# Another planned order of jobs for a three-layer block on one core: new seeds, other assumed transfer times

## The chip, the cores and the metric

The kernel runs on one core of one Trainium2 chip. The metric is the device time of one execution in microseconds (us), as the median of several runs. TensorE is PE in the profile, VectorE is DVE, ScalarE is ACT, GpSimd is POOL and SyncE, which here only issues DMAs, is SP.

## What is computed

Three layers run one after the other on 4 batches of 576 positions. The first is masked attention with 8 heads of 64 (half of them see a window of 32 positions, the other half every 32nd position), the second a gated feed-forward layer with a shift by one position, the third a feed-forward layer with a convolution of width 3 and a sigmoid gate.

```python
attn = softmax(where(mask, q @ k.T / 8, -1e9)) @ v          # 4 batches x 8 heads, 576 x 64
x_prev = shift_by_one(x)
xk = mu_k * x + (1 - mu_k) * x_prev;  xr = mu_r * x + (1 - mu_r) * x_prev
x = sigmoid(xr @ w_r) * (relu(xk @ w_k) ** 2 @ w_v)         # 512 -> 1024 -> 512
h = relu(x @ w_in)
c = conv_w[0] * h[t-1] + conv_w[1] * h[t] + conv_w[2] * h[t+1]
out = (h * sigmoid(c)) @ w_out                              # 512 -> 1024 -> 512
```

The weights of layers two and three arrive as 64-bit floats.

## The kernel before

Every matrix product is made of passes of 128 x 128 weights against 288 columns (half a batch, called a chunk; there are 8). For accuracy each operand is split into a high and a low part, and a product takes three passes instead of one. The weights are read as 64-bit words in pieces of 512 KB (tiles `raw`), which ScalarE or VectorE narrow to 32 bits (`wb`, `wt`, lines 407 to 418) and split (`wkh`, `wkl` and so on, lines 457 and 458).

There are two stages, and each is planned and emitted as a whole. In the first stage attention of batch b (scores `sc`, line 590; maximum and mask on VectorE, line 606; exponentials on ScalarE, line 611; turning the probabilities with TensorE, `tr`, lines 634 and 644; values `pv`, lines 667 and 676) stands beside the products of layer two (`mm`, line 785, with weights `wr`, `wk`, `wv`). Beside this the weights of layer three are prepared: read, narrowed, combined for a scheme with seven products in place of eight, split into `ws` (lines 471 and 472) and stored to DRAM (`wi_d`, `wo_d`). The results of layer two are split into `xo` (lines 852 and 853) and stored to DRAM too (`x_d`). In the second stage layer three runs: products `hh` (line 1038) from blocks `x` that are loaded back, and products `oz` and `ov` (line 1135).

Buffers are few: 2 of `raw`, 3 of `ws`, 2 of `xo`. An operation that writes into a `ws` or `xo` waits until the transfer out of the same buffer's earlier content has landed; an operation that reads `raw` waits for its transfer in. VectorE and ScalarE work through their instructions strictly in the order in which they were emitted, so what stands behind such a waiting operation waits too.

That order is set by a planner in the kernel file, which runs when the program is built. `Plan.run` (line 249) goes through the jobs with a list of estimated costs: at each step it takes the job that can start first, with ties broken by a rank. For a transfer it uses one line of estimated time with a fixed latency and a rate (line 316):

```python
dma = max(dma, t + DMA_LATENCY) + j.nbytes / DMA_RATE
j.end = dma
```

`Plan.search` (line 231) starts from ranks that follow the longest path, and then applies a fixed chain of seeds (the table `STEPS`, one tuple for each stage); each seed moves the ranks of some jobs by pseudo-random amounts (`vary`, line 191). The order of the last plan is what is emitted, and with it which of ScalarE and VectorE does a job that both can do. Where the plan has TensorE idle for over 0.48 us in its first 60 us, filling passes are emitted that compute nothing of use (`stir`, line 952): as many as `int((idle - 0.3) / 0.17)`, or `/ 0.26` near the start (line 292). `COLD` is the time until which the planner counts TensorE as slow.

The names of tiles in the order listings below carry a number where two words meet, as in `x_1_5969`; the number rises with the place of the job in the plan, and a higher one is a later job.

Of the kernel before, what the change touches and what calls it, by code (L numbers as in the profile page):

```python
# [26 lines left out]
BANKS = {"sc": 2, "tr": 2, "pv": 1, "mm": 3}  # L27
WARM, MIXES, BEHIND = 10, 2, (0, 3)
REBIAS = 2.0 ** -112
DMA_RATE, DMA_LATENCY = 365.0e3, 2.0  # L30
FOREVER = 1.0e9
PREFER, PREFER_FROM, BESIDE = 0.5, 20.0, 0.3
QUEUE, FEED = 64, 0.0142
CHUNK, AHEAD, FETCH, CROWD = 256, 85, 4.4, (0.4, 6.0)
GAP = {("mm", "half"): 0.09, ("tr", "half"): 0.17, ("tr", "tr"): 0.08}
ENTER = {("half", "mm"): 0.11, ("tr", "mm"): 0.085, ("half", "tr"): 0.05}
STEPS = ((30100000002, 30100000004, 30100000014, 30100000016, 30100000078, 30100000091, 30100000108, 30100000115, 30100000116, 30100000143,
# [9 lines left out]
HALF_ARRAY = {"sc", "pv"}  # L47
BLOCKS = ("B11", "B21", "B22", "T4", "T1", "T2", "T3")
WEIGHTS = ("A11", "A12", "A22", "S3", "S4", "S1", "S2")
# [7 lines left out]
SCRATCH = 1024  # L57
TAIL = 20.0
LQ, LK, LW, LB, LEAD = 64, 64, 96, (5, 4), 3
STIR_UNTIL, COLD = 60.0, 6.0  # L60
BANKED = {"sc", "tr", "pv", "mm"}
RIGHT = {"raw", "ws", "wt", "wb", "qk", "vt", "pr", "nmx", "sums", "rec", "pt"}
LATENCY = {"PE": 0.22, "ACT": 0.16, "DVE": 0.12, "POOL": 0.12, "SP": 0.0}
# [273 lines left out]
def block_kernel(ctx, tc, qkL, qkS, vL, vW, vS, mu_k, mu_r, w_k, w_v, w_r, w_in, conv_w, w_out, ident, mask_l, mask_w, mask_s, out):  # L337
# [612 lines left out]
    def stir(n, into, anew=True):  # L950
        for _ in range(n):
            pe.matmul(into[:, :T], idle[:, :P], idle, start=anew, stop=anew)
# [46 lines left out]
    def issue(stirred=False):  # L999
        plan.stirred = stirred  # L1000
        with tc.manual_schedule():
            if stirred:
                stir(WARM, scrap)
            for job, e, start, end in plan.search(START if stirred else SECOND, STEPS[not stirred]):
                if e == "PE":
# [282 lines left out]
```

## Time and profile before

| | |
|---|---|
| median of 3 runs | 515.7 us (513.41 to 516.38) |
| time of the profiled execution | 515.84 us |
| its span on the chip | 514.1 us |
| TensorE busy | 97% of the span |
| VectorE busy | 83% |
| ScalarE busy | 76% |
| moved by DMA | 96.61 MB, mean 188 GB/s |

The time of the profiled execution is 1.74 us longer than its span, for what lies around the span. Busy time says that an engine holds an instruction. TensorE is the engine nearly always busy, so the reading starts from the few places where it is not, and goes from each of them back to what released it.

### The profile page before, as it was taken

How to read it: one execution, taken by the hardware profiler on the slowest of the kernel's cores; microseconds unless marked ns; L12 is line 12 of the kernel's file. 1: busy time of each engine (PE TensorE's matmuls, PEld its weight loads, DVE VectorE, ACT ScalarE, POOL GpSimd, SP SyncE). 2: the span in 40 equal slices, each digit the busy share in tenths (PEclk: the TensorE clock that was granted, in tenths of full speed). 3: DMA queues.
4: the chain of work that ended last, by engine and by line, in shares of the span. 5: the costliest groups of instructions: out<-in, count | busy, mean ns of one | idle time of the engine just before them, and what ended most of it. 6: DMA issues, size and time to landing. Idle time of an engine off the chain costs nothing.

```text
span 514.1 us, 13571 instructions
## 1 busy us (share of the span) xinstructions
PE 498.6 (97%) x5123; PEld 480.7 (94%) x5123; DVE 424.9 (83%) x1195; ACT 390.6 (76%) x1140; POOL 1.1 (0%) x15
## 2 busy tenths in 40 slices
PE   8889999999999999999999999999999999999997
PEld 5679999899998899999899999999999999999997
DVE  4899899898946998977899613679999997897993
ACT  6999998999647999948979535377778667676762
POOL 0000000000000000000000000000000000000000
PEclk9999999999999999999999999999999999999999
DMA  8965575855676873797345997348109104610111
GB/s 289 368 197 158 171 242 181 283 199 193 206 241 210 328 254 126 244 311 254 132 165 205 364 312 250 118 170 292 42 13 345 46 25 160 219 38 1 47 48 69
DMA packets 57921, 96.61 MB, mean 188 GB/s; under 512 B 4864, under 2 KB 41984, under 8 KB 57600
## 3 DMA queue, kind: packets, MB, share of 16 engines
q1 hardware_dynamic: 57568, 95.58, 54.5%
q8 instruction: 40, 0.66, 0.6%
q14 instruction: 25, 0.20, 0.1%
q10 hardware_dynamic: 288, 0.16, 0.1%
HBM read 63.95 MB, written 31.78 MB: 186 GB/s over the span
## 4 chain that ended last, share of the span: by engine, by line
PE 56%; DMA 17%; ACT 14%; DVE 10%; issue 2%; SPq 0%; DVEq 0%; ACTq 0%
PE mm L785 22%; PE hh L1038 15%; PE oz L1135 10%; PE ov L1135 7%; DMA wi_d<-ws 3%; DMA wo_d<-ws 3%; DMA x_d<-xo 2%; ACT pr L611 2%; DMA raw<-in_w_r 2%; DMA raw<-in_w_v 2%; ACT mx L764 1%; DMA vt<-in_vW 1%; ACT wb L407 1%; DVE ws L472 1%; DMA x<-x_d 1%
## 5 line engine op out<-in xcount | busy, mean ns | idle before, releaser
L785 PE MATMUL mm<-X,wvh 128*128 128x288 f32 x448 | 83.2, 297 | 0.0
L1038 PE MATMUL hh<-x,wi 128*128 128x288 f32 x504 | 76.0, 297 | 1.4 <-DMA x<-x_d 0.7
L1038 PEld LDWEIGHTS hh<-x,wi 128*128 128x128 f32 x504 | 69.8, 188 | 2.8 <-DVE hb L1050 0.9
L785 PE MATMUL mm<-Y,wkh 128*128 128x288 f32 x384 | 69.0, 296 | 0.2 <-DVE sq L815 0.2
L785 PEld LDWEIGHTS mm<-X,wvh 128*128 128x128 f32 x448 | 66.7, 188 | 0.3
L611 ACT ACTIVATE pr<-pr,nmx 128x54 f32<-128x54 f32 (+2 forms) x160 | 53.6, 346 | 4.8 <-DVE nmx L606 4.8
L785 PEld LDWEIGHTS mm<-Y,wkh 128*128 128x128 f32 x384 | 56.5, 188 | 0.7 <-DVE sq L815 0.4
L785 PE MATMUL mm<-Y,wrh 128*128 128x288 f32 x256 | 55.2, 298 | 1.0 <-ACT rs L797 1.0
L1092 DVE SCALAR_TENSOR_TENSOR graw<-hb,cw_sb,graw 128x576 f32<-128x576 f32 x64 | 51.5, 812 | 1.6 <-ACT graw L1087 1.0
L1110 ACT ACTIVATE blk<-graw 128x576 fp32r<-128x576 f32 x56 | 37.4, 681 | 14.9 <-DVE graw L1094 4.1
L785 PE MATMUL mm<-X,wvl 128*128 128x288 f32 x224 | 47.9, 295 | 0.0
L1111 DVE TENSOR_TENSOR blk<-graw,blk 128x576 fp32r<-128x576 f32 x56 | 41.5, 752 | 6.0 <-ACT blk L1110 5.5
L785 PEld LDWEIGHTS mm<-Y,wrh 128*128 128x128 f32 x256 | 42.2, 188 | 1.7 <-ACT rs L797 1.5
L785 PE MATMUL mm<-Y,wkl 128*128 128x288 f32 x192 | 40.9, 294 | 0.0
L785 PE MATMUL mm<-Y,wrl 128*128 128x288 f32 x128 | 37.9, 296 | 0.3 <-DVE wrl L458 0.3
L826 DVE TENSOR_TENSOR X<-sq,X 128x288 fp32r<-128x288 f32 x48 | 21.5, 454 | 18.8 <-ACT X L824 14.9
L785 PEld LDWEIGHTS mm<-X,wvl 128*128 128x128 f32 x224 | 35.9, 188 | 0.0
L611 ACT ACTIVATION_READ_ACCUMULATOR pr<-pr,nmx 128x1 f32 x160 | 32.0, 200 | 0.0
L785 PEld LDWEIGHTS mm<-Y,wkl 128*128 128x128 f32 x192 | 30.6, 188 | 0.0
L1135 PE MATMUL oz<-blk,wo 128*128 128x288 f32 x192 | 30.1, 296 | 0.0
L808 ACT ACTIVATE rl<-mm 128x288 f32<-128x288 f32 x64 | 25.3, 404 | 6.3 <-PE mm L785 5.3
L472 DVE TENSOR_TENSOR ws<-wt,ws 128x512 fp32r<-128x512 f32 (+1 forms) x32 | 19.8, 619 | 9.9 <-DMA wi_d<-ws 5.4
(162 smaller groups left out, 1240.4 us busy)
## 6 DMA issues: line engine op xcount, KB each, us to landing
x_d<-xo SPq DMA_DIRECT2D x42, 288.0 KB, 2.5
x<-x_d SPq DMA_DIRECT2D x21, 576.0 KB, 6.0
wi_d<-ws SPq DMA_DIRECT2D x24, 256.0 KB, 4.0
wo_d<-ws SPq DMA_DIRECT2D x24, 256.0 KB, 2.6
wi<-wi_d SPq DMA_DIRECT2D x6, 896.0 KB, 7.8
qk<-in_qkS SPq DMA_DIRECT2D x8, 599.0 KB, 5.1
out<-ob SPq DMA_DIRECT2D x32, 144.0 KB, 1.7
qk<-in_qkL SPq DMA_DIRECT2D x7, 592.0 KB, 5.9
```

Source lines behind the costliest of these rows:

```text
L407: act.activation(b(), hw, AF.Copy, scale=REBIAS)
L472: plan.add({"DVE": 0.07 + n / 960}, lambda e: dve.tensor_tensor(lo()[:, :n], t()[:, k], hi()[:, :n].bitcast(F32), ALU.subtract), [t, hi], ...
L611: act.activation(pr()[:, k], pr()[:, k], AF.Exp, bias=nmx()[:, i:i + 1], scale=-1.0, accum_out=sums()[:, i:i + 1])
L764: plan.add({"ACT": 0.225 + n_ / 1400}, lambda e, v=v, t=t: act.activation(v(), x()[:, t, 1 + o:1 + o + n_], AF.Copy, scale=mu[:, t:t + 1]) ...
L785: pe.matmul(o(), w_cols(name, j, t, part), x_[t](), start=(t == 0 and part == 0 and x_ is xhi), stop=(t == nk - 1 and x_ is xlo))
L808: plan.add({"ACT": 0.295}, lambda e: act.activation(r(), o(), AF.Relu), [o], [r])
L826: plan.add({"DVE": 0.37}, lambda e: dve.tensor_tensor(l_(), sq(), h_().bitcast(F32), ALU.subtract), [sq, h_], [l_])
L1038: pe.matmul(o(), w(hw, j), x()[:, hx, j], start=anew and n == 0 and j == 0, stop=last and n == 2 and j == 1, skip_group_check=True)
L1092: plan.add({"DVE": 0.735}, lambda e, k=k: dve.scalar_tensor_tensor(c(), h()[:, k:k + S], cw_sb[:, k * NF + f:k * NF + f + 1], c(), ALU.mul ...
L1110: plan.add({"ACT": 0.13 + S / 1400}, lambda e, w=w, x=x: act.activation(w()[:, 0], x(), AF.Copy), [mine], [(w, 0)])
L1111: plan.add({"DVE": 0.07 + S / 960}, lambda e, w=w, x=x: dve.tensor_tensor(w()[:, 1], x(), w()[:, 0].bitcast(F32), ALU.subtract), [mine, (w ...
L1135: pe.matmul(o(), w_[s_][1](hw, q), x_()[:, hx, s_], start=anew and m == 0 and i == 0 and s_ == 0, stop=last and m == 1 and i == 2 and s_ = ...
```

## The change

Only numbers change. Three constants of the planner's costs are other ones: a transfer is now counted as one us later and at a rate 4% lower, and the slow time at the start as 7 us instead of 6. The table of seeds `STEPS` is replaced as a whole: 61 seeds become 93 for the first stage, and 26 become 34 for the second. They were chosen as those with which the plan ends first on the mean of eight cases with scattered transfer times, where the seeds before came from one plan. No operation is added to or taken from the computation; the order on each engine, the engine of some copies and the number of filling passes come out otherwise.

```diff
-DMA_RATE, DMA_LATENCY = 365.0e3, 2.0
+DMA_RATE, DMA_LATENCY = 350.0e3, 3.0
...
-STEPS = ((30100000002, 30100000004, 30100000014, 30100000016, 30100000078, 30100000091, 30100000108, 30100000115, 30100000116, 30100000143,
+STEPS = ((40300000007, 40300000026, 40300000031, 40300000050, 40300000114, 40300000121, 40300000163, 40300000246, 40300000278, 40300000284,
...
-STIR_UNTIL, COLD = 60.0, 6.0
+STIR_UNTIL, COLD = 60.0, 7.0
```

The table takes four more lines, so a line of the changed kernel stands 4 lines further down (L785 is now L789). The filling passes behind the ten at the start are 41 before and 32 now. ScalarE narrows 34 pieces of weights instead of 29 (the others are VectorE's), and gives nine short copies out of PSUM to VectorE.

The first place is TensorE in the opening, where the products with `wr` begin. Before, the scores of a unit of batch 1 (`sc<-qk 32x64`) stand among them with a run of filling passes behind (`L952`):

```order
L785 MATMUL mm<-Y_108,wrh_510 128x288
L785 MATMUL mm<-Y_108,wrl_576 128x288
L785 MATMUL mm<-Y_109,wrh_510 128x288
L590 MATMUL sc<-qk 32x64 x20
L952 LDWEIGHTS idle
L952 MATMUL mm<-idle 128x288
...
L785 MATMUL mm<-Y_104,wrh_752 128x288
L785 MATMUL mm<-Y_104,wrl_757 128x288
L785 MATMUL mm<-Y_105,wrh_752 128x288
```

Now the products go on with a shorter run of filling passes and no scores there:

```order
L789 MATMUL mm<-Y_106,wrh_629 128x288
L789 MATMUL mm<-Y_106,wrl_651 128x288
L789 MATMUL mm<-Y_107,wrh_629 128x288
L956 LDWEIGHTS idle
L956 MATMUL mm<-idle 128x288
...
L789 MATMUL mm<-Y_108,wrh_629 128x288
L789 MATMUL mm<-Y_108,wrl_651 128x288
L789 MATMUL mm<-Y_109,wrh_629 128x288
...
L789 MATMUL mm<-Y_104,wrh_684 128x288
L789 MATMUL mm<-Y_104,wrl_703 128x288
L789 MATMUL mm<-Y_105,wrh_684 128x288
```

Seven passes stood in the run of before; four and one stand in the two runs now. Of batch 1, three units' scores (14 blocks) stood ahead of the end of the `wr` products, and one unit's (5 blocks) does now; the other two follow among the `wk` and `wv` products.

The second place is VectorE where batch 2's first unit with strided heads is masked (`ms_sb`). Before, three writes into `ws` and the combinations `wt` stand ahead of the mask:

```order
L472 TENSOR_TENSOR ws<-wt,ws 128x512
L477 TENSOR_TENSOR wt<-wt 128x256
L826 TENSOR_TENSOR X_101<-sq,X_100 128x288
L826 TENSOR_TENSOR X_103<-sq,X_102 128x288
L472 TENSOR_TENSOR ws<-wt,ws 128x256
L477 TENSOR_TENSOR wt<-wt 128x256 x2
L826 TENSOR_TENSOR X_97<-sq,X_96 128x288
L477 TENSOR_TENSOR wt<-wt 128x256
L472 TENSOR_TENSOR ws<-wt,ws 128x512
L606 ISA pr,nmx<-sc,ms_sb 128x54
L606 ISA nmx 128x1
```

Now the write of 256 columns stands behind the whole unit (the rows left out are the other five blocks of the mask):

```order
L476 TENSOR_TENSOR ws<-wt,ws 128x512
L481 TENSOR_TENSOR wt<-wt 128x256
L830 TENSOR_TENSOR X_101<-sq,X_100 128x288
L830 TENSOR_TENSOR X_103<-sq,X_102 128x288
L840 SCALAR_TENSOR_TENSOR rs<-rs,mm 128x288
L610 ISA pr,nmx<-sc,ms_sb 128x54
L610 ISA nmx 128x1
...
L861 TENSOR_TENSOR rs<-rs 128x288
L476 TENSOR_TENSOR ws<-wt,ws 128x256
L481 TENSOR_TENSOR wt<-wt 128x256 x2
```

What moved is the `ws` of 256 columns and the combinations `wt` behind it, from ahead of the mask to behind it. On TensorE, 18 passes stood between this unit's scores and those of the next unit, which use the same two banks; 132 stand there now.

The third place is TensorE in the second stage, where the second batch of `hh` begins. The block `x_1` of the first batch is used for the last time, and the new one (a higher number) for the first time. Before:

```order
L1038 MATMUL hh<-x_1_5271,wrl__5326 128x288 x6
L1038 MATMUL hh<-x_6_5647,wrl__5365 128x288 x6
L1038 MATMUL hh<-x_4_5614,wrl__5383 128x288 x6
L1038 MATMUL hh<-x_0_5924,wi_5209 128x288 x6
L1038 MATMUL hh<-x_2_5637,wrh__5378 128x288 x6
L1135 MATMUL oz<-blk,wkh__5416 128x288
...
L1038 MATMUL hh<-x_5_5957,wi_5209 128x288 x6
L1038 MATMUL hh<-x_1_5969,wi_5209 128x288 x6
```

Now:

```order
L1042 MATMUL hh<-x_1_5447,wrl__5317 128x288 x6
L1042 MATMUL hh<-x_6_5638,wrl__5334 128x288 x6
L1042 MATMUL hh<-x_4_5605,wrl__5348 128x288 x6
L1139 MATMUL oz<-blk,wkh__5386 128x288
...
L1042 MATMUL hh<-x_2_5628,wrh__5353 128x288 x6
L1042 MATMUL hh<-x_0_5914,wi_5427 128x288 x6
L1139 MATMUL oz<-blk,wkh__5386 128x288
...
L1042 MATMUL hh<-x_5_5938,wi_5427 128x288 x6
L1042 MATMUL hh<-x_3_5658,wrh__5329 128x288 x6
L1042 MATMUL hh<-x_1_5960,wi_5427 128x288 x6
```

Between the last use of the old `x_1` and the first of the new one stood 36 passes, and stand 48 now, since two groups of six `oz` passes instead of one, and one more `hh` product, lie between them.

## Rows read from the trace of the kernel before

**Rows 1.** page of the profile: busy time of the engines, granted TensorE clock in 40 slices

```profile
PE 498.6 (97%) x5123; PEld 480.7 (94%) x5123; DVE 424.9 (83%) x1195; ACT 390.6 (76%) x1140; POOL 1.1 (0%) x15
PEclk9999999999999999999999999999999999999999
```

**Rows 2.** timeline of TensorE: start us, us, operation, count [idle before, releaser]

```profile
36.91 0.41 PE L785 MATMUL mm<-Y,wrh 128*128 128x288 f32 x1 [0.61 <-ACT rs L797]
...
69.42 0.55 PE L644 MATMUL tr<-id_sb,pr 128*128 128x128 f32 x3 [0.85 <-DVE pr L622]
...
95.37 0.27 PE L676 MATMUL pv<-pt,vt 54*64 54x54 f32 x2 [1.07 <-ACT xo L852]
...
165.58 0.85 PE L590 MATMUL sc<-qk 64*64 64x54 f32 x20 [0.97 <-DVE nmx L606]
...
192.47 0.40 PE L785 MATMUL mm<-Y,wrh 128*128 128x288 f32 x1 [0.41 <-ACT rs L797]
...
248.93 0.27 PE L676 MATMUL pv<-pt,vt 54*64 54x54 f32 x2 [0.95 <-ACT pt L653]
...
355.73 1.03 PE L1038 MATMUL hh<-x,wi 128*128 128x288 f32 x6 [0.70 <-DMA x<-x_d]
```

**Rows 3.** timeline of TensorE: filling passes at the start and in the opening

```profile
1.12 2.58 PE L952 MATMUL scrap<-idle 128*128 128x288 bf16 x10 [1.12 <-POOL xT L720]
...
32.34 1.03 PE L952 MATMUL mm<-idle 128*128 128x288 bf16 x7
```

**Rows 4.** timeline of VectorE: operations held up by a transfer

```profile
35.97 0.46 DVE L414 TENSOR_SCALAR wt<-raw 128x512 uint16<-128x512 uint16 x1 [0.96 <-DMA raw<-in_w_r]
...
68.20 0.46 DVE L414 TENSOR_SCALAR wt<-raw 128x512 uint16<-128x512 uint16 x1 [0.36 <-DMA raw<-in_w_v]
...
94.07 0.46 DVE L414 TENSOR_SCALAR wt<-raw 128x512 uint16<-128x512 uint16 x1 [0.78 <-DMA raw<-in_w_in]
...
162.38 0.42 DVE L472 TENSOR_TENSOR ws<-wt,ws 128x256 fp32r<-128x256 f32 x1 [1.53 <-DMA wi_d<-ws]
...
244.50 0.43 DVE L409 TENSOR_SCALAR wb<-raw 128x512 f32<-128x512 f32 x1 [1.18 <-DMA raw<-in_w_out]
```

**Rows 5.** timeline of ScalarE: an operation held up by a transfer

```profile
190.16 0.44 ACT L852 ACTIVATE xo<-rs 128x288 fp32r<-128x288 f32 x1 [0.36 <-DMA x_d<-xo]
```

**Rows 6.** DMA issues: out<-in, count, KB each, median us from issue to landing

```profile
x_d<-xo SPq DMA_DIRECT2D x42, 288.0 KB, 2.5
x<-x_d SPq DMA_DIRECT2D x21, 576.0 KB, 6.0
wi_d<-ws SPq DMA_DIRECT2D x24, 256.0 KB, 4.0
wo_d<-ws SPq DMA_DIRECT2D x24, 256.0 KB, 2.6
raw<-in_w_k SPq DMA_DIRECT2D x8, 512.0 KB, 3.7
raw<-in_w_v SPq DMA_DIRECT2D x8, 512.0 KB, 3.5
raw<-in_w_in SPq DMA_DIRECT2D x8, 512.0 KB, 5.0
raw<-in_w_out SPq DMA_DIRECT2D x8, 512.0 KB, 4.7
raw<-in_w_r SPq DMA_DIRECT2D x4, 512.0 KB, 6.3
```

**Rows 7.** chain that ended last, in order of time: start us, us, what

```profile
197.20 11.07 PE mm L785 x84
...
350.26 5.33 DMA x<-x_d
```

**Rows 8.** windows, all engines: PE, PEld, DVE, ACT, POOL busy us (count), clock, DMA

```profile
40.00:110.00 70.00, 68.00 (x904) 65.13 (x903) 65.31 (x234) 65.15 (x235) 0.11 (x1) 1.00 0.65 210
```

**Rows 9.** groups by shape, ScalarE exponentials: count, busy us, mean ns, idle before

```profile
L611 ACT ACTIVATE pr<-pr,nmx 128x64 f32<-128x64 f32 x54 | 18.2, 346 | 0.0
```

22 rows, old and new, of the table STEPS are left out of this document.

## The prediction

> **What bounds the kernel now.** [...] The passes themselves don't change, so the time can only move in what TensorE does beside them: waits, and the filling passes in the opening.
>
> The second view was the timeline of TensorE, for its idle times. Leaving out the start, the end and the small waits of the first 30 us, seven stand out: 0.61, 0.85, 1.07, 0.97, 0.41, 0.95 and 0.70 us, 5.56 together [rows 2]. The releasers named there are ScalarE and VectorE in six of the seven, so the third view was the timelines of those two engines just ahead of each wait. There the same thing is seen six times: an operation that had nothing to do with the waiting one stood ahead of it in the queue and was itself held up by a transfer. At 35.97 the first `wt` of a piece had waited 0.96 us for `raw`; at 68.20, 94.07 and 244.50 it was `raw` again, for 0.36, 0.78 and 1.18 us; at 162.38 a write into `ws` had waited 1.53 us for the store from that buffer [rows 4], and at 190.16 on ScalarE a write into `xo` 0.36 us [rows 5]. The seventh wait, 0.70 us at 355.73, is for the transfer of `x` itself, issued at 350.26 and landed 5.33 us later [rows 2, 7]. So these 5.56 us are the price of transfers that took longer than the planner had allowed for, paid by way of strict queues.
>
> **The change part by part.** The sum is made against the profiled execution of 515.84 us, which is 0.14 us above the median of the runs shown.
>
> First, the filling passes. They stand where the plan has TensorE idle, so nine fewer of them say that the planned waits of the opening are shorter by at least that. Seven took 1.03 us [rows 3], or 0.147 each; nine make 1.3 us. At the slow level of the start, where ten took 2.58 us [rows 3], nine would be 2.3; if VectorE, ScalarE or the transfers bound the opening all the same, the passes are only replaced by idle time, and the gain is 0. [...] I take 1.3: what made the waits was work of batch 1 on ScalarE and VectorE, and that has moved away. Its price is known: 9 blocks of scores less ahead of the end of the `wr` products, and an exponential costs 18.2/54 = 0.34 us of ScalarE [rows 9], so 3.0 us.
>
> Second, the room that transfers have. Between the job that issues a transfer and the first job that needs it (or its buffer), I counted the passes of TensorE in either order, at 11.07/84 = 0.132 us a pass [rows 7], and set that against the median landing of its kind: 2.5 us for `xo`, 4.0 for `ws` to `wi_d`, 2.6 for `ws` to `wo_d`, 3.7, 3.5, 5.0, 4.7 and 6.3 for the five kinds of `raw` [rows 6]. Of 137 such pairs (36 `raw`, 61 `ws`, 40 `xo`) 24 have less room than that before, and the shortfalls add up to 28.1 us; in the changed order 15 have less, by 15.8 us in all. `ws` gives most of it: eight places and 12.0 us become four and 2.6. So 44% of the shortfall is gone. The six waits that go back to such transfers make 0.61 + 0.85 + 1.07 + 0.97 + 0.41 + 0.95 = 4.86 us [rows 2], and 44% of them is 2.1 us. The ends are 0 (other operations get behind the transfers that still fall short) and 4.86 (each of the six has gone). At the largest with a `ws`, 0.97 us at 165.58, the order shows it directly: the write of 256 columns now stands behind the mask of the unit, and TensorE has 132 passes instead of 18 until it needs the bank. Against that stand two pieces of `raw` that now have less room than any before: one of `w_v` with 2.3 us and one of `w_out` with 1.9. They are in the 15.8.
>
> [...] The medians of 4.0 us for a store of 256 KB and 5.0 us for a read of 512 KB are this trace's [rows 6]. [...]
>
> Third, `x` in the second stage. The order gives the new `x_1` 48 passes instead of 36 between the last use of the old block and its own first use: 6.3 us instead of 4.8. The transfer took 5.33 [rows 7], so the wait of 0.70 us goes, and 1.0 us of room is left. With the median of 6.0 us for these transfers [rows 6] it just goes too. I take 0.7; the ends are 0 and 0.7. At the two later changes of batch every block has 42 passes or more in either order, 5.5 us.
>
> Fourth, the five pieces that ScalarE narrows instead of VectorE, and the nine copies that go the other way. They are a few tenths each on engines that are busy for 83% and 76% [rows 1]; TensorE's passes cover them, and I take 0. Without cover they are part of the second rival.
>
> The sum: 1.3 + 2.1 + 0.7 = 4.1 us, and 515.84 - 4.1 = 511.7 us.
>
> **The rivals.** Rival one: the waits move and do not go. ScalarE and VectorE keep their strict queues, and a plan that is good on the mean of cases need not be good on this chip's transfers; then 2.1 becomes 0 and of the 1.3 a part is lost, and the time is 515.84 - 0.7 - 1.1 = 514.0 us, with 513.1 to 516.5 around it. For it speaks that 15 of the 24 places are left; against it that the six waits each have a known cause, and that the places where the worst of them stood have more room now.
>
> Rival two, on the other side: the two units of batch 1 that left the opening come back between 40 and 110 us, on a ScalarE that is idle there for only 70.00 - 65.15 = 4.85 us [rows 8]. They bring 3.0 us. If they stand ahead of the evictions of the `mm` banks and not in ScalarE's gaps, TensorE waits for those: 515.84 - 1.1 - 0.7 + 3.0 = 517.0 us, and 518.8 if nothing is won elsewhere. It decides from the point where TensorE is idle there for over 3 us; before, it was for 70.00 - 68.00 = 2.00 [rows 8]. Against it speaks that part of the 4.85 us were themselves waits for transfers.
>
> [...]
>
> **How the numbers follow.** Forecast 0.55, rival one 0.30, rival two 0.11, rival three 0.04. The forecast's own spread is 509.5 to 513.1. A measurement of this kernel can tell about 0.5% from no change, here 513.1 and 518.3 us. Faster by more than that: the forecast and little else, 0.56. Slower: a third of rival two, half of rival three and what I have not seen, 0.09. Within: 0.35. The range reaches down to 508.8, where all the planned waits are worth 2.3, nearly all of the six waits go and `x` too (515.84 - 2.3 - 4.0 - 0.7), and up to 516.6, which takes in rival one and the lower part of rival two.
>
> **What would show it.** Right: in the opening the `wr` products end earlier, by 1 us or more; between 60 and 260 us TensorE's idle time is about half, and the writes into `ws` on VectorE wait less than before for the stores; no wait for `x` near 355 us; fewer and shorter rows on ScalarE and VectorE that are released by `raw`. [...] The prediction is wrong as a whole if the time is above 513.1 us or if TensorE's idle time beyond the start and end has not fallen by 2 us.

## The result, and the profile after

The changed kernel takes 509.44 us (median of 6 runs, 508.57 to 511.05), the kernel before, run beside it, 516.04 us (6 runs, 513.41 to 519.28). The ratio is 0.9874 with an interval of 0.9836 to 0.9913: 6.6 us faster, where 4.1 were predicted. The profiled executions are 508.81 us with a span of 507.0, and 515.84 with 514.1. All medians and ratios below leave out the runs that fell into a slower state of the chip.

The two rows of the page that answer to [rows 1], busy time and granted clock of the changed kernel:

```profile
PE 498.2 (98%) x5114; PEld 480.6 (95%) x5114; DVE 426.0 (84%) x1198; ACT 390.0 (77%) x1137; POOL 1.6 (0%) x15
...
PEclk9999999999999999999999999999999999999999
```

TensorE does the same work in the same time (498.2 us against 498.6), in a span that is 7.1 us shorter. So the time came out of its idle stretches. The chain that ended last says the same; its shares by engine, first of the kernel before:

```profile
PE 56%; DMA 17%; ACT 14%; DVE 10%; issue 2%; SPq 0%; DVEq 0%; ACTq 0%
```

and of the changed kernel:

```profile
PE 88%; ACT 5%; DMA 4%; DVE 2%; issue 1%; SPq 0%; ACTq 0%
```

Transfers and the two engines that wait for them made 41% of the chain, and make 11% now. (The chain is one path, and its shares are not times that could be saved.) Where that happened is read from TensorE's timeline, the view of [rows 2]. These are all its waits behind the first 30 us in the changed kernel (start, length, operation, and in brackets the idle time before it with its releaser):

```profile
31.32 0.53 PE L789 MATMUL mm<-Y,wrh 128*128 128x288 f32 x2 [0.29 <-DVE Y L771]
...
32.65 0.40 PE L789 MATMUL mm<-Y,wrl 128*128 128x288 f32 x1 [0.26 <-DVE wrl L462]
...
35.44 0.40 PE L789 MATMUL mm<-Y,wrh 128*128 128x288 f32 x1 [0.28 <-ACT rs L801]
...
117.74 0.53 PE L789 MATMUL mm<-Y,wkh 128*128 128x288 f32 x2 [0.19 <-ACT rs L801]
...
327.38 7.45 PE L1042 MATMUL hh<-x,wi 128*128 128x288 f32 x54 [0.56 <-ACT b L1050]
...
335.36 4.26 PE L1042 MATMUL hh<-x,wi 128*128 128x288 f32 x30 [0.53 <-ACT a L1050]
```

Of the six waits behind transfers (4.86 us) one of 0.28 us is left (0.61 before, at 36.91); the other five have gone. Between 40 us and the second stage there were 5.21 us of waits in seven places, and there is one of 0.19. Five of the seven stand in [rows 2]; the other two of the kernel before, and one in its second stage that has no row there either, are these:

```profile
169.72 0.79 PE L590 MATMUL sc<-qk 64*64 64x54 f32 x22 [0.78 <-issue]
...
241.57 0.53 PE L785 MATMUL mm<-Y,wkh 128*128 128x288 f32 x2 [0.18 <-DVE sq L815]
...
334.04 6.25 PE L1038 MATMUL hh<-x,wi 128*128 128x288 f32 x45 [0.50 <-ACT b L1046]
```

For the 0.78 us at 169.72 the trace names no releaser ("issue"). The windows show the change as busy time. Of 60 to 260 us, first the kernel before (PE, PEld, DVE, ACT, POOL busy us, then clock, DMA share and GB/s):

```profile
60.00:260.00 200.00, 194.60 (x2545) 186.81 (x2544) 172.19 (x624) 168.68 (x605) 0.21 (x2) 1.00 0.67 225
```

and the changed kernel, with the window that answers to [rows 8]:

```profile
40.00:110.00 70.00, 70.00 (x950) 67.31 (x949) 65.30 (x239) 62.98 (x214) 0.62 (x1) 1.00 0.68 222
60.00:260.00 200.00, 199.79 (x2623) 192.24 (x2622) 169.68 (x623) 170.52 (x603) 0.72 (x2) 1.00 0.65 218
```

TensorE's idle time between 60 and 260 us fell from 5.40 us to 0.21.

Three marks cut the span: the first `wkh` product starts at 44.99 before and 43.51 after, the first `hh` at 328.79 and 322.08. So the opening is 1.48 us shorter, the stretch from there to the second stage 5.23 (283.80 to 278.57), and the second stage 0.39. I call that stretch the middle; most of what follows is about it. The three stretches as windows, first of the kernel before, then of the changed one:

```profile
0.00:44.99 44.99, 39.44 (x610) 31.51 (x611) 35.91 (x173) 38.47 (x144) 0.62 (x7) 1.00 0.81 268
44.99:328.79 283.80, 278.32 (x3172) 270.02 (x3171) 226.05 (x753) 223.55 (x750) 0.48 (x8) 1.00 0.66 224
328.79:514.10 185.31, 180.85 (x1346) 179.19 (x1344) 162.98 (x270) 128.61 (x247) 0.00 (x0) 1.00 0.32 113
```

```profile
0.00:43.51 43.51, 39.09 (x529) 30.69 (x529) 36.30 (x163) 37.77 (x142) 0.62 (x7) 1.00 0.78 263
43.51:322.08 278.57, 278.37 (x3245) 270.56 (x3243) 227.31 (x766) 225.85 (x749) 0.99 (x8) 1.00 0.68 230
322.08:507.00 184.92, 180.72 (x1346) 179.31 (x1344) 162.38 (x270) 126.41 (x247) 0.00 (x0) 1.00 0.33 114
```

The marks don't cut off the same work: 81 passes fewer stand in the opening now (most of them scores that moved, and nine filling passes), and 73 more in the middle. TensorE's idle time, length less busy time, leaves the moved work out: it fell from 5.55 to 4.42 us in the opening, from 5.48 to 0.20 in the middle and from 4.46 to 4.20 in the second stage.

The operations behind which these waits stood [rows 4, 5] are held less. The view of waits of ScalarE and VectorE in the middle (line, what it waited for, us in total, times, longest), the largest entries, first of the kernel before:

```profile
ACT xo L852 <- DMA x_d<-xo: 9.4, 9, 2.6
DVE ws L472 <- DMA wi_d<-ws: 5.4, 2, 3.9
ACT wb L407 <- DMA raw<-in_w_in: 4.4, 4, 1.4
ACT wb L407 <- DMA raw<-in_w_v: 3.0, 3, 2.2
```

and of the changed kernel:

```profile
ACT xo L856 <- DMA x_d<-xo: 9.0, 7, 5.3
DVE ws L476 <- DMA wi_d<-ws: 4.5, 3, 3.4
ACT wb L411 <- DMA raw<-in_w_v: 1.4, 1, 1.4
...
ACT wb L411 <- DMA raw<-in_w_in: 0.4, 1, 0.4
```

The reads of weights give most of the difference: summed over all entries, what was held behind `raw` fell from 15.0 us to 3.9, behind `ws` from 9.7 to 6.1, and behind `xo` hardly, from 9.4 to 9.0. One write into `xo` was still held for 5.3 us, and TensorE has no wait that answers to it: this hold cost nothing, since TensorE had products to run all the while.

Transfers themselves did not become faster as a whole. Their medians in the changed kernel, which answer to [rows 6]:

```profile
x_d<-xo SPq DMA_DIRECT2D x42, 288.0 KB, 3.2
...
wi_d<-ws SPq DMA_DIRECT2D x24, 256.0 KB, 3.7
wo_d<-ws SPq DMA_DIRECT2D x24, 256.0 KB, 2.9
...
raw<-in_w_in SPq DMA_DIRECT2D x8, 512.0 KB, 4.6
```

### The profile page after: what moved, and what is told of

The parts are those of the page before. It is cut to its first block, busy times and chain, and to the rows that moved or that the text cites. A ratio compares the mean times of both kernels' runs of the same rounds, so it can differ in the third digit from the quotient of the medians.

```text
span 507.0 us, 13536 instructions
## 1 busy us (share of the span) xinstructions
PE 498.2 (98%) x5114; PEld 480.6 (95%) x5114; DVE 426.0 (84%) x1198; ACT 390.0 (77%) x1137; POOL 1.6 (0%) x15
## 4 chain that ended last, share of the span: by engine, by line
PE 88%; ACT 5%; DMA 4%; DVE 2%; issue 1%; SPq 0%; ACTq 0%
PE mm L789 47%; PE hh L1042 17%; PE oz L1139 10%; PE ov L1139 8%; PE sc L594 3%; DMA x_d<-xo 2%; PE pv L680 2%; PE tr L648 1%; DMA raw<-in_w_in 1%; ACT pr L615 1%; DMA qk<-in_qkL 1%; ACT wb L411 1%; ACT mx L768 1%; DVE pr L610 0%; ACT Y L770 0%
## 5 line engine op out<-in xcount | busy, mean ns | idle before, releaser
L789 PE MATMUL mm<-X,wvh 128*128 128x288 f32 x448 | 84.5, 298 | 0.0
L789 PE MATMUL mm<-Y,wkh 128*128 128x288 f32 x384 | 68.2, 295 | 0.2 <-ACT rs L801 0.2
L789 PEld LDWEIGHTS mm<-X,wvh 128*128 128x128 f32 x448 | 67.0, 188 | 0.3
L789 PEld LDWEIGHTS mm<-Y,wkh 128*128 128x128 f32 x384 | 56.4, 188 | 0.5 <-ACT rs L801 0.4
L789 PE MATMUL mm<-Y,wrh 128*128 128x288 f32 x256 | 55.9, 301 | 0.6 <-DVE Y L771 0.3
L789 PE MATMUL mm<-X,wvl 128*128 128x288 f32 x224 | 47.9, 295 | 0.0
L1114 ACT ACTIVATE blk<-graw 128x576 fp32r<-128x576 f32 x56 | 36.4, 678 | 11.1 <-DVE graw L1120 5.0
L789 PEld LDWEIGHTS mm<-Y,wrh 128*128 128x128 f32 x256 | 42.1, 188 | 1.9 <-DVE Y L771 0.8
L789 PE MATMUL mm<-Y,wkl 128*128 128x288 f32 x192 | 40.8, 294 | 0.0
L789 PE MATMUL mm<-Y,wrl 128*128 128x288 f32 x128 | 38.0, 297 | 0.3 <-DVE wrl L462 0.3
L789 PEld LDWEIGHTS mm<-X,wvl 128*128 128x128 f32 x224 | 35.9, 188 | 0.0
L789 PEld LDWEIGHTS mm<-Y,wkl 128*128 128x128 f32 x192 | 30.7, 188 | 0.0
L1097 ACT ACTIVATE graw<-graw 128x576 f32<-128x576 f32 x32 | 21.8, 681 | 9.8 <-DVE graw L1096 9.7
```

The costliest lines, as they stand in the source:

```text
L789: pe.matmul(o(), w_cols(name, j, t, part), x_[t](), start=(t == 0 and part == 0 and x_ is xhi), stop=(t == nk - 1 and x_ is xlo))
L1097: plan.add({"ACT": 0.6}, lambda e: act.activation(c(), c(), AF.Sigmoid), [mine], [mine], table="sigmoid")
L1114: plan.add({"ACT": 0.13 + S / 1400}, lambda e, w=w, x=x: act.activation(w()[:, 0], x(), AF.Copy), [mine], [(w, 0)])
```

## The experiments

The theory after the result: the changed plan gives transfers in the middle enough room, so that VectorE and ScalarE are seldom held by one for so long that TensorE notices. The rivals: the second stage or the opening gives the gain; the order around the held operations matters, not the planner's transfer time; any other plan would do as well; the filling passes.

**Which stage.** Two kernels join the first stage of one with the second of the other (the tables are shortened here).

```diff
-STEPS = ((30100000002, ...), (10100000007, ...))
+STEPS = ((40300000007, ...), (10100000007, ...))
+        DMA_RATE, DMA_LATENCY = (350.0e3, 3.0) if stirred else (365.0e3, 2.0)
```

(first_new, which also has `COLD` at 7; in second_new all is the other way round.)

> The changed first stage (its 93 seeds and the three constants) with the second stage of before (its 26 seeds, planned with the constants of before). Main theory: the gain is idle time of TensorE in the first stage that goes back to operations on VectorE and ScalarE held up by transfers, and nine filling passes less; in the two traces the first hh product starts 6.7 us earlier, and the second stage is only 0.4 us shorter. So the time is 509.8 us (509 to 511), and first hh starts near 322 us. Rival one: the first stage leaves its transfers or weights in a state that only the changed second stage makes use of; then a part of the 6.7 us is lost at the border and the time is 512 or more. Rival two: the gain comes from the second stage by the wait for x that went; then 515.3.

> The first stage of before with the changed second stage (34 seeds, new constants there). Main theory: 515.6 us, 0.4 less than before: the wait of 0.70 us for x at 355 goes, and new waits of about half a microsecond for ScalarE (b and a) take its place. Third step of the prediction (0.7 us from the second stage): 515.3. Rival: the second stage gives a part of the 6.6 us that the milestones hide, because it overlaps the end of the first; then 513 to 514.

Measured: 509.94 us for first_new (ratio to before 0.9879, 0.9834 to 0.9923) and 516.07 for second_new (1.0009, 0.9979 to 1.0038). The whole gain is in the first stage. In second_new no wait for `x` is left, and the one of 0.53 us for `a` has come.

**Moving operations out from behind the held ones.** hoist47 keeps plan, seeds and costs of before and changes the emitted order only.

```diff
-            for job, e, start, end in plan.search(START if stirred else SECOND, STEPS[not stirred]):
+            planned = plan.search(START if stirred else SECOND, STEPS[not stirred])
+            for job, e, start, end in (hoist(planned, 4.0, 0.15) if stirred else planned):
```

> The seeds and constants of before. The planned order of the first stage is changed after planning: 47 operations of attention on VectorE and ScalarE (masks, exponentials, sums, copies) that stood behind an operation that reads raw, or that opens a ws or xo buffer, are put ahead of it, where everything they need is planned to be ready by the held operation's own start. Only from 40 us on and by at most 4 us; TensorE keeps its order of products. Main theory (operations held by transfers in strict queues make TensorE wait): of the waits at 69.42, 95.37, 165.58 and 248.93, 0.85 + 1.07 + 0.97 + 0.95 = 3.84 us, half or more goes, and the time is 512.5 to 514.3 against 516.0. Rival: the waits depend on how the work of the engines is spread, not on what stands ahead of what; the time is then 515.5 or above, and above 517 if the moved operations delay the products' own evictions.

Measured: 524.14 us, ratio 1.0153 (1.0095 to 1.0211). The expectation failed, and in the wrong direction; the time lies where its rival put it, above 517. What happened at one place, in three rows of the timeline of all engines:

```profile
250.48 0.69 DVE L472 TENSOR_TENSOR ws<-wt,ws 128x512 fp32r<-128x512 f32 x1 [1.64 <-DMA wo_d<-ws]
...
253.03 0.45 ACT L813 ACTIVATE sq<-rl 128x288 f32<-128x288 f32 x1 [3.47 <-DVE X L826]
...
259.11 0.27 PE L676 MATMUL pv<-pt,vt 54*64 54x54 f32 x2 [2.05 <-ACT pt L653]
```

VectorE is still held by a store. The `X` behind it on VectorE is late, ScalarE waits 3.47 us for that, and TensorE in the end 2.05. Over the whole middle the time that VectorE and ScalarE are held by transfers fell only from 34.1 us to 31.4, and TensorE's waits rose from 5.2 to 8.6. My reading is that a mask that goes ahead of a narrowing makes the narrowing later, with it the split, its store, and the next write into that buffer, so that the waits move along the ring of buffers; no run shows this step by step. The run speaks neither for the theory nor clearly against it: the holds themselves were not taken away. What it shows is that these 47 moves by hand did not help.

**The constants and the seeds apart.** Seeds move ranks on top of what the plan found, so with other constants they lead to another plan, one that nobody chose. That makes four unchosen plans, two with each assumed transfer time. constants_only has the seeds of before and all three new constants in both stages; transfers_first only the transfer constants and only in the first stage; slow_start_first only `COLD` there; seeds_first has the new seeds and the old constants there.

```diff
 # constants_only
-DMA_RATE, DMA_LATENCY = 365.0e3, 2.0
+DMA_RATE, DMA_LATENCY = 350.0e3, 3.0
-STIR_UNTIL, COLD = 60.0, 6.0
+STIR_UNTIL, COLD = 60.0, 7.0
 # transfers_first
+        DMA_RATE, DMA_LATENCY = (350.0e3, 3.0) if stirred else (365.0e3, 2.0)
 # slow_start_first
-STIR_UNTIL, COLD = 60.0, 6.0
+STIR_UNTIL, COLD = 60.0, 7.0
 # seeds_first
-STEPS = ((30100000002, ...), (10100000007, ...))
+STEPS = ((40300000007, ...), (10100000007, ...))
```

> The seeds of before with the three new constants (a transfer counted one us later and 4% slower; slow start 7 us). The seeds move ranks by pseudo-random amounts on top of what the plan found, so the order comes out otherwise, with 46 filling passes behind the first ten instead of 41. Main theory: the gain needs both, room for transfers and seeds chosen for it; seeds that are not chosen for these costs leave TensorE idle where the plan itself has it idle: 516 to 522 us, with fewer waits behind raw, ws and xo but more for results of VectorE and ScalarE. Rival: the longer assumed transfers alone make the room: 511 to 513.5 us.

> The seeds of before; in the first stage only, a transfer is counted with 3.0 us and 350 instead of 2.0 and 365 (the slow start stays at 6 us); the second stage is that of before. Theory as revised after constants_only, whose first stage ended 4.2 us earlier and had one wait left beyond 40 us: the assumed transfer time alone makes the planner leave room, seeds chosen for it are not needed for that; first hh near 324 to 326 us, TensorE idle under 1.5 us between 40 us and there, time 511.5 to 513. Rival: that first stage was a chance of the seeds' pseudo-random moves, or came from the constant of the slow start; then 514 to 518, with waits behind raw, ws or xo again.

> The changed seeds with the transfer times and the slow start of before in the first stage; the second stage is that of before. Theory: without the longer assumed transfers the room goes, the seeds can't replace it; TensorE idle over 3 us between 40 us and the first hh, time 514 to 518. Rival: the seeds carry the gain of the first stage; 509.5 to 512.

> The seeds and transfer times of before, in the first stage only the slow start counted as 7 us instead of 6: seeds that are not chosen for their costs, but with the short assumed transfers. It is the control to transfers_first and constants_only, whose stretch from the first wkh product to the first hh took 281.1 and 279.1 us with unchosen seeds and long assumed transfers (before 283.8). Theory (the assumed transfer time makes the room): here that stretch takes 283.5 us or more, with waits behind raw, ws and xo, and the time is 516 to 522. Rival (any other plan is as good on average): that stretch is 279 to 281.5 us.

Measured against before: constants_only 520.51 us (1.0100, 1.0063 to 1.0136), transfers_first 516.38 (0.9997, 0.9970 to 1.0024), seeds_first 533.90 (1.0322, 1.0266 to 1.0378), slow_start_first 522.77 (1.0112, 1.0073 to 1.0151). By the totals, transfers_first went to its rival (its first `hh` came at 329.5 us, not at 324 to 326, and TensorE's waits before it were 2.2 us, not under 1.5), seeds_first is 16 us beyond its range, slow_start_first 0.8 us beyond, and constants_only lies in its range, with the waits for VectorE that were expected, but all at the end of the second stage. The totals mislead, since every plan also has an opening and an end of its own. The profiles taken apart at the marks, in us; "held" is the sum of all entries of VectorE and ScalarE in the view of waits that were ended by a transfer, "TensorE waits" the same sum of TensorE's entries, both in the middle:

| kernel | assumed transfer | seeds chosen for it | opening | middle | TensorE waits | held |
|---|---|---|---|---|---|---|
| before | 2.0 us, 365 | yes | 45.0 | 283.8 | 5.2 | 34.1 |
| slow_start_first | 2.0 us, 365 | no | 46.5 | 291.7 | 8.5 | 34.4 |
| seeds_first | 2.0 us, 365 | no | 47.1 | 300.4 | 12.4 | 33.4 |
| hoist47 | 2.0 us, 365 | moved by hand | 46.4 | 292.4 | 8.6 | 31.4 |
| transfers_first | 3.0 us, 350 | no | 48.3 | 281.1 | 2.2 | 14.6 |
| constants_only | 3.0 us, 350 | no | 45.5 | 279.1 | 0.4 | 9.8 |
| first_new | 3.0 us, 350 | yes | 45.1 | 278.1 | 0.0 | 16.8 |
| after | 3.0 us, 350 | yes | 43.5 | 278.6 | 0.2 | 19.5 |

The assumed transfer time splits the table: held 31 to 34 us with the short one, 10 to 20 with the long one, and no plan of one kind has a middle like the other. Both unchosen plans with the long time have a better middle than the chosen one of before. These are few plans: first_new and after run the same first stage, so three plans with the long time stand against three with the short one and the hand-moved hoist47. Waits are not all of a longer middle: in hoist47 it is 8.6 us longer than before with 3.4 us more of waits, and TensorE is busy there for 283.47 us against 278.32, in part with slower passes (the last section has rows; the mean granted clock of this execution was 0.993, that of before 0.999). What the old seeds lost under the new constants stands elsewhere. In transfers_first it is one wait in the opening; in constants_only it is VectorE in the end of the second stage, which a plan with these seeds leaves too much to do:

```profile
19.90 0.80 PE L678 MATMUL pv<-pt,vt 96*64 96x64 f32 x20 [2.40 <-DVE pt L405]
```

```profile
489.45 0.37 PE L1135 MATMUL ov<-blk,wkh__5446 128*128 128x288 f32 x1 [1.60 <-DVE ob L1154]
...
493.74 0.61 PE L1135 MATMUL ov<-blk,wkh__5446 128*128 128x288 f32 x1 [3.25 <-DVE ob L1154]
```

How one late transfer becomes a wait of TensorE is plainest in slow_start_first. The timeline of all engines there, with ScalarE and VectorE held by the same `raw`, and TensorE behind them:

```profile
105.45 0.68 ACT L418 ACTIVATE wb<-raw 128x512 f32<-128x512 f32 x1 [4.52 <-DMA raw<-in_w_in]
105.45 0.46 DVE L425 TENSOR_SCALAR wt<-raw 128x512 uint16<-128x512 uint16 x1 [3.58 <-DMA raw<-in_w_in]
...
107.57 0.65 PE L655 MATMUL tr<-id_sb,pr 118*118 118x118 f32 x2 [3.49 <-ACT xT L723]
```

**More load on the transfers.** Each of the 64 stores of split weights is done twice, the extra one ahead and into scratch memory (nothing reads it). In the first pair all extra stores go to one tensor, in the second each to its own (the lines that declare `again` and name the job `j` are left out).

```diff
 # before_twice, after_twice
+            j.emit = lambda e, f=j.emit, x=x: (nc.sync.dma_start(out=again[:, :n], in_=x()[:, :n].bitcast(F32)), f(e))
 # before_apart, after_apart
+            j.emit = lambda e, f=j.emit, x=x: (nc.sync.dma_start(out=again.pop()[:, :n], in_=x()[:, :n].bitcast(F32)), f(e))
```

> The kernel before; each store of split weights (ws to wi_d and wo_d) is preceded by the same store to a scratch tensor, so a ws buffer comes free later and the transfers behind it start later. The order of all else is unchanged. Theory: before has little room (24 of 137 pairs short), so most of what a transfer is later is a wait of TensorE: 519 to 524 us, 3 to 8 more than before. Rival: the waits of before have other causes than the landing time, or an in-order queue hides it: at most 1.5 us more.

> The changed kernel with the same doubled stores. Theory: it has more room (15 pairs short, by about half as much), so it loses less than before does: 510.5 to 513 us, 1 to 3.5 more than the changed kernel, and the distance to before_twice grows beyond 6.6 us to 8 or more. Rival: room has no part in the gain; both lose the same, and the distance stays at 6 to 7 us.

> The kernel before with each of the 64 stores of split weights done twice, now each extra store into a scratch tensor of its own. In before_twice all went to one tensor, and SyncE's queue stood 81 us waiting for the earlier scratch store; that stall is gone here, and what is left is that a ws buffer comes free later, by the time the second store takes beside the first. Theory (before has little room): 519 to 530 us, 3 to 13 more than before. Rival (room has no part): within 1.5 us of before.

> The changed kernel with the same 64 extra stores into tensors of their own. Theory (it has more room): it loses at most two thirds of what before loses, and the distance to before_apart is 8 us or more; 511 to 518 us. Rival: both lose alike, distance 5.5 to 7.5 us.

The first pair took 570.04 and 554.27 us (ratios to before 1.1023, 1.0971 to 1.1075, and 1.0703, 1.0654 to 1.0751), ten times the loss that I had expected and more. The view of waits of before_twice names the flaw, in SyncE's queue (total, times, longest):

```profile
SPq L477 <- DMA again<-ws: 81.2, 53, 5.6
```

The extra stores waited 53 times for an earlier one into the same tensor, 81.2 us in all, and SyncE's queue stood for that time. The second pair is free of that: 535.83 us (1.0370, 1.0334 to 1.0407) and 517.91 (1.0023, 0.9996 to 1.0049). Before loses 19 us, the changed kernel 8.5, and the distance grows from 6.6 to 17.9. Under the same load, held is 56.1 us in the middle of before_apart and 44.7 in after_apart, and TensorE's waits are 16.4 and 5.6. The loss is not waits alone: in the middle of before_apart TensorE was also busy for 286.49 us, 8.2 more than without the extra stores, and in after_apart for 281.06, 2.7 more. The size of the loss was again misjudged, for before_apart by 6 us beyond its range; that the changed plan loses less than half as much fits the room, and not its rival.

**The filling passes.** after_no_filling leaves out the 32 passes behind the first ten, which compute nothing of use.

```diff
-                        stir(job.idle, bank(), anew)
+                        stir(0, bank(), anew)
```

> The changed kernel without the 32 filling passes behind the first ten. Theory: they lie in TensorE's idle time; without them the opening waits just as long: 509 to 510.5 us, unchanged within 0.3%. First step of the prediction taken at its word (each pass is worth 0.147 us): 4.7 us faster, 504.7. Rival three: the granted clock falls in the opening: 511 us or more, with slices of it below the top tenth before 40 us.

Measured: 511.50 us, 0.9891 of before (0.9858 to 0.9924), against 0.9874 for the changed kernel; the intervals overlap. The first `wkh` product starts at 43.45 us against 43.51. Taking away 32 passes moved nothing there, as the theory has it. But the granted clock fell, as the rival has it, and the median is 2.1 us higher, which these runs can't tell from no difference. The windows of this kernel:

```profile
20.00:25.00 5.00, 2.94 (x101) 2.11 (x98) 5.00 (x24) 5.00 (x26) 0.00 (x0) 0.98 1.00 367
25.00:30.00 5.00, 3.97 (x53) 3.27 (x54) 4.73 (x16) 4.63 (x14) 0.00 (x0) 0.50 0.56 182
```

TensorE was busy for 2.94 of 5 us, and in the next 5 us the granted clock was 0.50; in the changed kernel TensorE was busy for 3.94 of the same 5 us, and the clock in the next 5 was 1.00. VectorE and ScalarE were busy for 5.00 us each of the first 5 and for 4.73 and 4.63 of the next. My reading is that they set the pace there, so that the clock cost little in this execution (509.03 us).

No version beat the changed kernel; first_new equals it.

## Why the prediction was right, and where its sizes were off

The direction and the mechanism were right: transfers that take longer than the planner allows for, paid by way of strict queues (in the middle of before, transfers held VectorE and ScalarE for 34.1 us, and TensorE waited 5.2), and a changed plan that gives them room. The sum was 2.5 us short, and the steps stand as follows.

First, the filling passes, 1.3 us. The opening did end 1.48 us earlier in the profiled execution, but this is not shown to be a gain. The same opening took 45.08 us in first_new, against 43.51 in the changed kernel: single executions of one order differ by as much as the gain. The step failed in reading fewer passes as shorter waits. The passes stand in time in which TensorE waits anyway, and without any of them the opening is as long (43.45 us in after_no_filling).

Second, the room, 2.1 us with ends 0 and 4.86: this is the term that was mis-sized. The six waits that it was made from gave 4.58 (4.86 less the 0.28 that is left). The middle as a whole gave 5.23 by the marks and 5.0 by its waits (5.21 less 0.19); in that are 0.78 and 0.18 us at 169.72 and 241.57, which the prediction had left out when it read the timeline, though the first is longer than three of its seven. The step failed where TensorE's waits were to fall by the same share as the shortfall, 44%: the six fell by 94%. That the time held by transfers fell by nearly that share, from 34.1 us to 19.5 or 43%, is luck in good part. The count had `ws` give 9.4 of the 12.3 us of shortfall that go; measured, `ws` gave 3.6 of the 14.6 us and `raw` 11.1. And executions of this one first stage differ (19.5 us, 16.8 in first_new, and 16.0 in after_no_filling, which lacks the filling passes).

Why 43% less of held time took nearly all of the waits is argued and not shown: a hold reaches TensorE only when it outlasts the products that TensorE has queued, and the 5.3 us at `xo` did not. The sum of held time by itself does not fix the waits. At 31 to 34 us held, four kernels have 5.2 to 12.4 us of them, and after_apart has 5.6 at 44.7 us held. The case that stood at the lower end of the range, that nearly all of the six waits go, is the one that came.

Third, `x`, 0.7 us. The wait at 355.73 went, but the second stage gave only 0.39 us, and second_new as a whole no gain that can be measured: a wait of 0.53 us for ScalarE's `a` took the place, 13 us after the first `hh` instead of 27. A wait of 0.50 us for `b` at 334.04, which the prediction had not listed, stayed (0.56 now).

Fourth, the moved narrowings and copies, 0: nothing in the profile speaks against it. ScalarE and VectorE are 77% and 84% busy, one point more each in a shorter span.

Rival one (the waits move and do not go) fell: 0.19 us are left in the middle. Rival two (batch 1 comes back at 40 to 110 us) fell: TensorE is busy there for 70.00 of 70.00 us. Rival three (0.04 by the prediction) is a granted clock that falls in the opening when filling passes are fewer. It did not happen in the changed kernel, whose granted clock is in the top tenth in all 40 slices. But the clock does fall in the opening in two other runs: in after_no_filling to 0.50 at 25 to 30 us, and in the profiled execution of first_new, which has the same first stage and all 32 passes, to 0.66 at 15 to 20 us.

```profile
10.00:15.00 5.00, 3.75 (x85) 2.83 (x77) 3.42 (x27) 3.95 (x22) 0.00 (x0) 1.00 0.69 159
15.00:20.00 5.00, 4.51 (x59) 3.53 (x59) 4.24 (x23) 4.51 (x23) 0.00 (x0) 0.66 1.02 373
```

That the slices of before are in the top tenth also where TensorE was idle for 2.12 us of 12.85 (the first two slices) does not speak against this rival, then. Nor does the row of the clock tell of every slow pass: it reads 1.00 from 1.10 to 3.70 us of the kernel before, where ten filling passes took 0.258 us each instead of 0.147.

What stays open: the choice of seeds on the mean of eight cases was not tested by itself, nor were the latency of 3.0 us and the rate of 350 apart. That the longer assumed transfer time makes the middle is shown by three plans against three and by a pair under load; that the seeds are needed for an opening and a second stage that lose nothing is shown by two plans only. More buffers for `ws`, `xo` or `raw`, which would test the room most directly, were not tried.

## What to carry to other kernels

Where a planner writes a fixed order for strict queues, look at the transfer time that it assumes before its search: here one us more and a rate 4% lower made the middle 3 to 6 us shorter in three plans, but only with seeds chosen for these costs was the whole kernel faster. Don't expect the waits of the bounding engine to fall in proportion to the room that a plan lacks: here a plan with 44% less of a shortfall lost 94% of the waits put down to it. Check also which transfers give the change, and not the total alone. Don't judge a part of a plan by the total of one variant; cut the span at marks, and compare stretch with stretch.

## What the runs showed of the hardware that was not expected

A wait of TensorE was paid twice in second_new: the wait before 95.92 was 1.87 us, where before had 1.07 at the same place, and the granted clock was 0.52 in the 3 us behind it. The windows around it (TensorE's busy time first, the granted clock third from the end):

```profile
93.00:96.00 3.00, 1.13 (x14) 0.93 (x15) 1.51 (x9) 1.93 (x10) 0.00 (x0) 1.00 0.99 352
96.00:99.00 3.00, 3.00 (x35) 2.87 (x35) 2.00 (x15) 2.48 (x14) 0.00 (x0) 0.52 0.40 153
99.00:102.00 3.00, 3.00 (x73) 2.69 (x73) 1.75 (x7) 2.10 (x9) 0.00 (x0) 0.92 0.74 247
```

In hoist47 products behind two waits took longer: four passes of one kind took 0.69 us ahead of the waits of 0.88 and 1.32 us (at 169.27) and 1.16 us behind them (at 176.53), in TensorE's timeline:

```profile
169.27 0.69 PE L785 MATMUL mm<-X,wvh 128*128 128x288 f32 x4
...
176.53 1.16 PE L785 MATMUL mm<-X,wvh 128*128 128x288 f32 x4
```

The length of the wait alone does not decide whether the clock falls. In the same kernel the wait of 2.05 us at 259.11, longer than those above, left the clock at 1.00:

```profile
256.00:259.00 3.00, 1.06 (x9) 0.82 (x7) 2.17 (x8) 3.00 (x13) 0.00 (x0) 1.00 0.02 5
259.00:262.00 3.00, 2.89 (x43) 2.84 (x44) 2.38 (x16) 2.79 (x15) 0.00 (x0) 1.00 0.08 22
```

So did one of 2.11 us at 239.11 in after_apart, whose mean granted clock is 1.000. What decides between them these runs don't show.

A lower granted clock goes with a part of the scatter. Of 51 runs of the kernel before, taken beside the experiments, 21 had a mean granted clock below 0.999, with a median of 517.1 us, and the other 30 a median of 516.0. All six runs of the changed kernel were at 0.999 or above. They lie within 2.5 us of each other, where the six of before taken beside them lie within 5.9; that the room is the cause of this is not shown.
